# Weight loads moved behind a transpose, mixing ahead of the next products, and reciprocals on ScalarE, in a planned attention and GLU block

## Chip, cores and metric

The kernel runs on one core of a Trainium2 chip. The metric is the device time of one execution in microseconds (us); the time before is 262.38 us, the median of 3 runs (262.22 to 262.53).

## What is computed

```python
xn = layernorm(x)                                  # x: 2048 x 640
q, k, v = split_heads(xn @ wqkv)                   # 32 heads of 20
logits[h, s, w] = q[h, s] . k[h, s - 2 w] / sqrt(20), w = 0..7, masked where s < 2 w
attn = softmax(logits, axis=w)
o[h, s] = sum_w attn[h, s, w] * v[h, s - 2 w]
out = x + o @ wo + ((xn @ w_gate) * (xn @ w_up)) @ w_down   # 1536 hidden
```

All inputs and the output are bf16. Every position looks at eight positions only, so the attention itself is elementwise work and not a matrix product.

## The kernel before

The 2048 positions are cut into four chunks of 512 (c = 0 to 3). Features lie on the partitions, 5 tiles of 128; the 512 positions of a chunk are the free dimension. All matmuls of the projections, the gate/up part and the output are 128x128 weights against 128x512.

**Normalized input.** Chunk 0 takes a short way: its x comes in already turned, in two halves of 256 positions (`load_x0`, L139), TensorE sums over features with a matrix of ones (`feature_sums`, L246), VectorE subtracts the mean (`center`, L263), ScalarE squares (`squares`, L273) and takes the root by Ln and Exp (`roots`, L282), and the q and k projections run on the centered x and are scaled afterwards (`first`, L301). Chunks 1 to 3 come in row by row: VectorE takes the statistics (`stats`, L203), GpSimd the inverse root (L221 to L224), ScalarE scales (L233), SP stores the result xn in DRAM (`keep_xn`, L374) and reads it back with a DMA that transposes it into `xnT` (`turn_all`, L381).

**Projections** (`project`, L416): 10 groups of 5 matmuls give q and k, 5 groups give v; ScalarE casts each from PSUM (L450). k and v keep a halo of 14 positions of the chunk before, copied by GpSimd (L439).

**Gate and up** (`glu`, L667): per chunk 12 tiles f, each a gate group and an up group of 5 matmuls; ScalarE casts both (L679) and VectorE multiplies them to h(c, f) (L693).

**Attention** (`attention`, L634). VectorE multiplies q with k shifted, two offsets at a time (n = 0 to 3; `product`, L494), and adds five tiles to one (`fold`, L505 to L508). Two folds make one group g of four offsets: TensorE sums over the features of a head with a 128x32 matrix (`logits`, L520), ScalarE takes the exponential (`exps`, L529) into e, SP stores e in DRAM (`keep_e`, L541) and loads it back spread over the features of each head, as A(c, g) (`load_a`, L553). TensorE sums e over the offsets (`sums`, L565), VectorE takes the reciprocal (`inverse`, L577), and SP spreads it by way of DRAM as R(c). VectorE mixes: A times shifted v (`mix`, L608), added up (`gather`, L618), folded and multiplied with R to o(c) (`whole`, L626, L627).

**Down and output** (`finish`, L701): for each of 5 output tiles, 12 matmuls of w_down with all h(c, f) and 5 of wo with o(c) into one PSUM bank (L713, L718); VectorE adds x (L735), and GpSimd, in the last chunk SP, stores (L740). For chunk 3 all five down groups come first and the outputs after them.

**Order of the work.** Nothing is scheduled at run time. Each engine runs one list in order, and the class `Plan` (L27) makes these lists when the program is built. Every step is added with its engine, a cost in us that the author put down, the steps that it needs, a priority (lower first), rings (how many buffers there are, and which step frees one) and a slack added to its ready time. `run` (L56) takes, again and again, the engine that can start first and the ready step of lowest priority on it. A step on the same engine becomes ready `LAG` (0.2) after the end of what it needs. So a cost or a priority changes only the order in which instructions stand on an engine. The DMA issues of SP, ScalarE and GpSimd stand in the lists of these engines, and an engine that waits for a semaphore holds up everything behind it in its list.

Weights are loaded in blocks, `wa` and `wqkv` by SP and ScalarE (L167 to L177), `wgu`, `wd` and `wo` by GpSimd; each GpSimd load is held back by a tiny copy that reads one element of something earlier (`gate`, L183).

Of the kernel before, what the change touches and what calls it, by code (L numbers as in the profile page):

```python
# [7 lines left out]
BF = dt.bfloat16  # L8
# [18 lines left out]
class Plan:  # L27
# [8 lines left out]
    def __init__(self, rings):  # L36
        self.rings = {n: (k, []) for n, k in rings.items()}
        self.tasks = {e: [] for e in ("pe", "dve", "act", "pool", "sp")}
        self.done = {}
        self.start = {}  # L40
        self.free = {"pe": 2.9, "dve": 0.8, "act": 0.81, "pool": 1.6, "sp": 0.8}
        self.dma = 2.0
# [3 lines left out]

    def ready(self, t):
        _, _, name, _, _, need, ring, _, _, slack = t
        r = max((self.done.get(n, self.INF) for n in need), default=0.0) + slack
        for one in (ring,) if isinstance(ring, str) else ring or ():  # L50
            k, users = self.rings[one]
            if len(users) >= k:
                r = max(r, self.done.get(users[-k], self.INF))
        return r

    def run(self):  # L56
        while any(self.tasks.values()):
            best = None
            for e, ts in self.tasks.items():
                if not ts:  # L60
                    continue
                rs = [(self.ready(t), t) for t in ts]
# [12 lines left out]
            emit()  # L75
            self.start[name] = at
            self.free[e] = at + took
            self.done[name] = at + took + self.LAG
            if kb is not None:
                self.dma = max(self.dma, at + took + 0.7) + kb / 360.0  # L80
                self.done[name] = self.dma + 1.0
# [3 lines left out]
def tile_kernel(ctx: ExitStack, tc, x, xT, x0_in, wa_in, wqkv_in, wo_in, wgu_in, wd_in, sel_in, out):  # L85
# [37 lines left out]
    def warm_up(n):  # L123
        for _ in range(n):
            nc.tensor.matmul(wps[:, 0:P], lhsT=warm[:], rhs=warm[:], start=True, stop=True)

    warm_up(19)

    plan = Plan({"mm": 5, "lg": 1, "aux": 2, "pw": 1, "f": 4, "m": 2, "q": 2, "xnT": 2, "h": 24, "g": 4,
                 "xt": 6, "A": 1, "o": 1, "xr": 3, "osb": 4, "xn": 1})  # L130
    add = plan.add
    st = {c: {} for c in range(NCH)}

# [5 lines left out]
    def load_x0(eng, h, lo, hi):  # L139
        def emit():  # L140
            if (h, lo) == (0, 0):
                both = pool.tile([P, 2, KT, CS], BF, name="x0", tag="m", bufs=2)
                st[0]["xt"], st[0]["xd"] = both[:, 0], both[:, 1]
            eng.dma_start(out=st[0]["xt"][:, lo:hi, h * CS // 2 : (h + 1) * CS // 2], in_=x0_in[h, :, lo:hi, :])

        return emit
# [20 lines left out]
    for eng, q, name, dst, src, cut, kb in (  # L167
# [6 lines left out]
        ("sp", nc.sync, ("wb", 0), wqkv, wqkv_in, blocks(0, 2), 320),  # L174
        ("act", nc.scalar, ("wb", 2), wqkv, wqkv_in, blocks(2, 5), 480),
        ("sp", nc.sync, ("wv",), wqkv, wqkv_in, blocks(5, 10), 800),
# [20 lines left out]
    add("pool", ("wgu", 6), gated(wgu, wgu_in, blocks(6, FT), lambda: wqkv[:, 9, KT - 1, P - 1 :]), 1.2, [("wv",)], prio=order, kb=1920); order += 1  # L197
    add("pool", ("wd",), gated(wd, wd_in, slice(None), lambda: st[0]["f", 0][:, 0, 0:1]), 1.2, [("pw", 0, 0)], prio=order, kb=1920); order += 1
    add("pool", ("wo",), gated(wo, wo_in, slice(None)), 1.1, [("wd",)], prio=order, kb=800); order += 1
# [46 lines left out]
    def feature_sums(what, h, lo, hi):  # L246


        def emit():
            if lo == 0:  # L250
                st[0]["sum", what, h] = ps_aux.tile([P, CS // 2], F32, name="sum_" + what, tag="aux")
            a, b = HALVES[h]
            for i in range(lo, hi):
                nc.tensor.matmul(
                    st[0]["sum", what, h][:], lhsT=ones[:], rhs=st[0][what][:, i, a:b],
                    start=(i == 0), stop=(i == KT - 1),
                )
            if what == "xt" and h == 0:
                warm_up(6 if hi == KT else 2)

        return emit

    def center(h, lo, hi):  # L263
        def emit():
            a, b = HALVES[h]
            nc.vector.scalar_tensor_tensor(
                st[0]["xd"][:, lo:hi, a:b], wide(st[0]["sum", "xt", h][:], hi - lo), -1.0 / D,
                st[0]["xt"][:, lo:hi, a:b], op0=ALU.mult, op1=ALU.add,
            )

        return emit

    def squares(h, lo, hi):  # L273
        def emit():
            if (h, lo) == (0, 0):
                st[0]["sq"] = pool.tile([P, KT, CS], BF, name="sq", tag="o", bufs=1)
            a, b = HALVES[h]
            nc.scalar.activation(st[0]["sq"][:, lo:hi, a:b], st[0]["xd"][:, lo:hi, a:b], ACT.Square)

# [10 lines left out]
    def normalized(h):  # L290
        def emit():
            if h == 0:
                st[0]["xnT"] = pool.tile([P, KT, CS], BF, name="xnT", bufs=2)
            a, b = HALVES[h]
            nc.vector.tensor_tensor(  # L295
                st[0]["xnT"][:, :, a:b], st[0]["xd"][:, :, a:b], wide(rstd0[:, a:b], KT), ALU.mult
            )
# [3 lines left out]
    def first(h, j, hi, i=None):  # L301


        def emit():
            if i == 0 or (i is None and h == 1):
                st[0]["ps0", j] = ps_main.tile([P, 2, CS // 2], F32, name="ps0", tag="mm")
            a, b = HALVES[h]
            for n in range(2):
                for ii in range(KT) if i is None else (i,):
                    if (h == 0 and (i is None) == (n == 0)):  # L310
                        continue
                    nc.tensor.matmul(
                        st[0]["ps0", j][:, n, :], lhsT=(wqkv[:, j, ii, :] if n else wa[:, ii, j, :]),
                        rhs=st[0]["xd"][:, ii, a:b], start=(ii == 0), stop=(ii == KT - 1), skip_group_check=True,
                    )
# [72 lines left out]
    for c in range(1, NCH):  # L388
# [3 lines left out]
        for k in ks:  # L392
            add("dve", ("stats", c, k), stats(c, k), 1.1, [("xc", c), ("xn0", 1)], prio=c * 100 - 110)
        add("pool", ("root", c), root_pool(c, ks), 2.2, [("stats", c, k) for k in ks], prio=c * 100)
# [239 lines left out]
    def attention(c, prio, mprio):  # L634
        halves = ((0, CS // 2), (CS // 2, CS)) if c == 0 else ((0, CS),)
        for n in range(W // 2):
            g = n // 2
            for lo, hi in halves:
                add("dve", ("pwh", c, n, lo), product(c, n, lo, hi), 2 * KT * (hi - lo) / 1920 + 0.08,
                    [("qk", c, lo)] + ([("pwh", c, n, 0)] if lo else []), prio=prio + (n if lo == 0 else n),  # L640
                    ring=("pw" if lo == 0 else None), until=("pw", c, n))
            add("dve", ("pw", c, n), fold(c, n), 2.3, [("pwh", c, n, halves[-1][0])], prio=prio + n - 0.5, ring="f", until=("logits", c, g))
        for g in range(2):
            add("pe", ("logits", c, g), logits(c, g), 0.3, [("pw", c, 2 * g + 1), ("pw", c, 2 * g), ("sel",)], prio=-100,
                ring="lg", until=("exp", c, g))
            add("act", ("exp", c, g), exps(c, g), 0.6, [("logits", c, g)], prio=-100)
            if c == 0 and g == 1:
# [4 lines left out]
                ring="A" if g == 0 else None, until=("m", c, W // 2 - 1))  # L652
        add("pe", ("sums", c), sums(c), 0.15, [("exp", c, 0), ("exp", c, 1)] + ([("mask", c)] if c == 0 else []), prio=-100,
            ring="aux", until=("rs", c))
        add("dve", ("rs", c), inverse(c), 1.3, [("sums", c)], prio=-50)
        add("sp", ("kept r", c), keep_r(c), 0.65, [("rs", c)], prio=-100, kb=64)
        add("sp", ("R", c), load_r(c), 0.65, [("kept r", c)] + ([("o", c - 1)] if c else []), prio=-100, kb=128)
        for n in range(W // 2):
            add("dve", ("m", c, n), mix(c, n), 2.75, [("A", c, n // 2), ("v", c)], prio=mprio + n,
                ring="m", until=("mm", c, n + 1) if n < W // 2 - 1 else ("o", c))  # L660
            if n:
                add("dve", ("mm", c, n), gather(c, n), 2.75, [("m", c, n)], prio=mprio + n)
        add("dve", ("o", c), whole(c), 2.85, [("mm", c, W // 2 - 1), ("R", c)], prio=mprio + 9, ring="o", until=("pe fin", c, KT - 1))

# [36 lines left out]
    def finish(c, prio):  # L701
        for m in range(KT):
# [68 lines left out]
    for c in range(NCH):  # L771
# [4 lines left out]
        finish(c, 500 + 100 * c)  # L776
        attention(c, 100 * c, 100 * c + 150)
    plan.run()
# [56 lines left out]
```

## Time and profile before

| | |
|---|---|
| median of 3 runs | 262.38 us |
| the profiled execution's own time | 261.74 us |
| its span, first to last instruction | 260.0 us |
| granted TensorE clock over the span | 1.0 |
| VectorE busy | 229.8 us |
| ScalarE busy | 104.6 us |
| DMA | 27.10 MB, mean 104 GB/s |
| mean of a 128x512 gate/up matmul (L673) | 379 ns, one every 216 ns |
| product (L494), mix (L608), gather (L618), each 128x5120 | 2.8 us |
| reciprocal (L577) | 951 ns, 4 times |

All times inside the execution are microseconds from the start of the span. In the rows of the timeline the first number is the start, the second the time from the first start to the last end of the merged instructions, then engine, line, operation, tiles and shape, the count, and in brackets the idle time before it with what ended it. PE is TensorE's matmuls, PEld its weight loads, DVE VectorE, ACT ScalarE, POOL GpSimd, SP the engine that only issues DMAs. In the rows of a group, the numbers after the bar are busy time and mean duration, and after the second bar the idle time before. Matmuls overlap, so their durations don't add up; the starts do.

### The profile page before, as it was taken

What the parts mean: (1) busy time and instruction counts of PE and PEld (TensorE: products, weight loads), DVE (VectorE), ACT (ScalarE), POOL (GpSimd) and SP (SyncE); (2) the same over time, 40 slices, a digit from 0 to 9 for tenths busy, and PEclk for the clock granted to TensorE, in tenths of its full rate; (3) what the DMA queues carried; (4) which work ended last, traced back from release to release, by engine and by line L of the source; (5) the groups of instructions that cost most, each with busy time, mean ns of one, the idle gap of its engine ahead of it and who ended that gap; (6) DMA issues with size and microseconds to landing.
All of it is one profiled execution on the core that took longest, in us unless ns stands there. A gap on an engine that the chain in (4) does not pass through costs nothing.

```text
span 260.0 us, 3329 instructions
## 1 busy us (share of the span) xinstructions
PE 253.0 (97%) x1275; PEld 121.6 (47%) x1298; DVE 229.8 (88%) x235; ACT 104.6 (40%) x178; POOL 37.8 (15%) x67
## 2 busy tenths in 40 slices
PE   8999999999999999999999999999999999999994
PEld 6784444434444444444444444444444444444462
DVE  2599789972999999999999999999999989999813
ACT  3415595559555564525045645520035554000000
POOL 0302800022100000317040002003040000031000
PEclk9999999999999999999999999999999999999999
DMA  6993198305650000511540001502115004020002
GB/s 217 402 426 147 33 347 281 75 24 199 218 91 16 7 0 24 191 55 65 182 107 12 1 25 35 190 20 77 45 49 179 2 13 151 20 81 40 23 0 101
DMA packets 17503, 27.10 MB, mean 104 GB/s; under 512 B 9584, under 2 KB 13296, under 8 KB 17104
## 3 DMA queue, kind: packets, MB, share of 16 engines
q1 hardware_dynamic: 13664, 14.18, 17.3%
q0 software_dynamic: 2336, 11.31, 11.8%
q10 hardware_dynamic: 1488, 1.41, 1.6%
q8 instruction: 10, 0.16, 0.3%
q14 instruction: 5, 0.04, 0.1%
HBM read 19.16 MB, written 5.77 MB: 96 GB/s over the span
## 4 chain that ended last, share of the span: by engine, by line
PE 84%; DVE 6%; DMA 3%; POOL 2%; ACT 2%; issue 1%; ACTq 1%
PE psf L713 20%; PE ps L429 19%; PE psu L673 17%; PE psg L673 17%; PE psf L718 8%; DMA wqkv<-wqkv 3%; PE lps L520 1%; DVE stats L210 1%; DVE xnT L295 1%; POOL rstd L222 1%; ACT x_c L233 1%; DVE pw L494 1%; POOL rstd L221 1%; DVE q L331 0%; DVE k L331 0%
## 5 line engine op out<-in xcount | busy, mean ns | idle before, releaser
L673 PEld LDWEIGHTS <-wgu 128*128 128x128 bf16 x480 | 46.6, 98 | 56.5 <-issue 0.7
L673 PE MATMUL psu<-xnT,wgu 128*128 128x512 bf16 x234 | 59.3, 379 | 0.3
L673 PE MATMUL psg<-xnT,wgu 128*128 128x512 bf16 x235 | 59.4, 379 | 0.3
L713 PE MATMUL psf<-hT,wd 128*128 128x512 bf16 (+1 forms) x246 | 54.1, 369 | 0.3
L608 DVE TENSOR_TENSOR m<-v,A 128x5120 bf16<-128x5120 bf16 x16 | 44.9, 2814 | 6.0 <-DMA A<-eD 6.0
L494 DVE TENSOR_TENSOR pw<-q,k 128x5120 bf16<-128x5120 bf16 (+1 forms) x20 | 45.6, 2284 | 0.0
L679 ACT CAST us<-psu 128x512 bf16<-128x512 f32 x48 | 28.1, 586 | 31.1 <-PE psu L673 30.9
L429 PE MATMUL ps<-xnT,wqkv 128*128 128x512 bf16 x170 | 40.0, 379 | 0.3
L679 ACT CAST gs<-psg 128x512 bf16<-128x512 f32 x48 | 28.2, 587 | 27.5 <-PE psg L673 27.5
L713 PEld LDWEIGHTS <-wd 128*128 128x128 bf16 x252 | 24.6, 98 | 27.4 <-issue 0.2
L618 DVE TENSOR_TENSOR m<-m 128x5120 bf16<-128x5120 bf16 x12 | 33.8, 2817 | 0.0
L429 PEld LDWEIGHTS <-wqkv 128*128 128x128 bf16 x175 | 17.0, 98 | 20.4 <-issue 0.2
L718 PE MATMUL psf<-o,wo 128*128 128x512 bf16 (+1 forms) x104 | 24.2, 369 | 0.1
L693 DVE TENSOR_TENSOR hT<-gs,us 128x512 bf16<-128x512 bf16 x48 | 19.6, 418 | 3.3 <-ACT us L679 3.2
L740 POOL DMA_DIRECT2D out<-osb x15 | 8.2, 549 | 78.5 <-DVE osb L735 78.2
L505 DVE TENSOR_TENSOR pw<-pw 128x2048 bf16<-128x2048 bf16 x16 | 19.5, 1217 | 0.0
L429 PE MATMUL ps<-xnT,wa 128*128 128x512 bf16 x75 | 18.5, 380 | 0.0
L450 ACT CAST v<-ps 128x512 bf16<-128x512 f32 x20 | 11.6, 586 | 14.0 <-PE ps L429 14.0
L718 PEld LDWEIGHTS <-wo 128*128 128x128 bf16 x105 | 10.3, 98 | 11.3
L233 ACT ACTIVATE x_c<-x_c,mrstd,rstd 128x640 bf16<-128x640 bf16 x12 | 10.8, 922 | 9.3 <-POOL mrstd L224 9.3
L450 ACT CAST q<-ps 128x512 bf16<-128x512 f32 x15 | 8.8, 584 | 7.5 <-PE ps L429 7.5
L506 DVE TENSOR_TENSOR pw<-pw 128x1024 bf16<-128x1024 bf16 x16 | 11.1, 692 | 0.5
(85 smaller groups left out, 170.2 us busy)
## 6 DMA issues: line engine op xcount, KB each, us to landing
A<-eD SPq DMA_DIRECT2D x8, 512.0 KB, 4.5
x_c<-x SPq DMA_DIRECT2D x3, 640.0 KB, 8.5
wgu<-wgu POOLq DMA_DIRECT2D x1, 1920.0 KB, 11.1
wd<-wd POOLq DMA_DIRECT2D x1, 1920.0 KB, 8.8
xnD<-x_c SPq DMA_DIRECT2D x3, 640.0 KB, 5.4
xr<-xT POOLq DMA_DIRECT2D x15, 128.0 KB, 4.2
out<-osb POOLq DMA_DIRECT2D x15, 128.0 KB, 2.0
wgu<-wgu POOLq DMA_DIRECT2D x1, 1280.0 KB, 7.3
```

The lines of the kernel that those rows point to most:

```text
L233: nc.scalar.activation(st[c]["x", k], st[c]["x", k], ACT.Identity, bias=b, scale=r)
L429: nc.tensor.matmul(ps[:, 0 : hi - lo], lhsT=weight(b, i), rhs=s["xnT"][:, i, lo:hi], start=(i == 0), stop=(i == KT - 1),)
L450: nc.scalar.copy(dst[:, t, o + lo : o + hi], s["ps", b, lo][:, 0 : hi - lo])
L494: nc.vector.tensor_tensor(s["pw", n][:, :, :, lo:hi], s["q"][:, None, :, lo:hi].to_broadcast([P, 2, KT, hi - lo]), pairs(s["k"][:, :, off ...
L505: nc.vector.tensor_tensor(t[:, :, 0:2, :], t[:, :, 0:2, :], t[:, :, 2:4, :], ALU.add)
L608: nc.vector.tensor_tensor(s["m", n][:], pairs(s["v"][:, :, off : off + CS], DIL), s["A"][:, 2 * n : 2 * n + 2, None, :].to_broadcast([P, 2 ...
L618: nc.vector.tensor_tensor(b[:], a[:], b[:], ALU.add)
L673: nc.tensor.matmul(ps[:], lhsT=wgu[:, f, r, i, :], rhs=st[c]["xnT"][:, i, :], start=(i == 0), stop=(i == KT - 1))
L679: nc.scalar.copy(t[:], st[c]["gps", f, r][:])
L693: nc.vector.tensor_tensor(h[:], st[c]["gu", f, 0][:], st[c]["gu", f, 1][:], ALU.mult)
L713: nc.tensor.matmul(ps[:], lhsT=wd[:, f, m * P : (m + 1) * P], rhs=st[c]["h", f][:, lo:hi], start=(f == 0), stop=False)
L718: nc.tensor.matmul(st[c]["psf", m, lo][:], lhsT=wo[:, t, m * P : (m + 1) * P], rhs=st[c]["o"][:, t, lo:hi], start=False, stop=(t == KT - 1))
```

## The change

1. The first half and the second half of chunk 0's x, of its centered form and of its squares each get a tile of their own, so that a row of a half is contiguous; before, a half was a strided part of a row of 512.
2. The load of block 2 to 4 of `wqkv` moves from ScalarE's queue to SP's, and there are 22 warm-up matmuls instead of 19.
3. The load of `wd` waits for the transpose of chunk 1 (`turned`) instead of chunk 0's first fold; `wo` follows it.
4. Mixing of chunks 0 to 2 gets a priority ahead of the products of the next chunk (100 c + 50 instead of 100 c + 150, where the next chunk's products have 100 c + 100).
5. The reciprocal of the sums becomes exp(-ln(s)) by two ScalarE activations instead of a VectorE reciprocal.
6. In the planner, logits get a slack of 0.8 and sums one of 0.6; several costs are raised; a step that needs one on its own engine isn't charged the lag; statistics of chunks 2 and 3 get a later priority; the last chunk's down waits in the plan for the end of chunk 2's output; two entries are put into ring "m".

```diff
-    def ready(self, t):
+    def ready(self, e, t):
...
-        r = max((self.done.get(n, self.INF) for n in need), default=0.0) + slack
+        r = max((self.done.get(n, self.INF) - (self.LAG if self.by.get(n) == e else 0.0) for n in need), default=0.0) + slack
...
-    warm_up(19)
+    warm_up(22)
...
+    plan.rings["m"][1].extend([("xn0", 1), ("kept", 1)])
...
-                both = pool.tile([P, 2, KT, CS], BF, name="x0", tag="m", bufs=2)
-                st[0]["xt"], st[0]["xd"] = both[:, 0], both[:, 1]
-            eng.dma_start(out=st[0]["xt"][:, lo:hi, h * CS // 2 : (h + 1) * CS // 2], in_=x0_in[h, :, lo:hi, :])
+                both = pool.tile([P, 2, 2, KT, CS // 2], BF, name="x0", tag="m", bufs=2)
+                for n in range(2):
+                    st[0]["xt", n], st[0]["xd", n] = both[:, 0, n], both[:, 1, n]
+            eng.dma_start(out=st[0]["xt", h][:, lo:hi, :], in_=x0_in[h, :, lo:hi, :])
...
-        ("act", nc.scalar, ("wb", 2), wqkv, wqkv_in, blocks(2, 5), 480),
+        ("sp", nc.sync, ("wb", 2), wqkv, wqkv_in, blocks(2, 5), 480),
...
-    add("pool", ("wd",), gated(wd, wd_in, slice(None), lambda: st[0]["f", 0][:, 0, 0:1]), 1.2, [("pw", 0, 0)], prio=order, kb=1920); order += 1
+    add("pool", ("wd",), gated(wd, wd_in, slice(None), lambda: st[1]["xnT"][:, KT - 1, CS - 1 :]), 1.2, [("turned", 1)], prio=order, kb=1920); order += 1
...
-            add("dve", ("stats", c, k), stats(c, k), 1.1, [("xc", c), ("xn0", 1)], prio=c * 100 - 110)
+            add("dve", ("stats", c, k), stats(c, k), 1.05, [("xc", c), ("xn0", 1)], prio=c * 100 - 180 if c > 1 else -10)
...
+            l = pool.tile([P, P], F32, name="ls", bufs=1)
             r = pool.tile([P, P], BF, name="rs", bufs=1)
-            with nc.allow_low_precision(reason="weights are bf16"):
-                nc.vector.reciprocal(r[:], st[c]["sps"][:])
+            nc.scalar.activation(l[:], st[c]["sps"][:], ACT.Ln)
+            nc.scalar.activation(r[:], l[:], ACT.Exp, scale=-1.0)
...
-            add("dve", ("pw", c, n), fold(c, n), 2.3, [("pwh", c, n, halves[-1][0])], prio=prio + n - 0.5, ring="f", until=("logits", c, g))
+            add("dve", ("pw", c, n), fold(c, n), 2.55, [("pwh", c, n, halves[-1][0])], prio=prio + n - 0.5, ring="f", until=("logits", c, g))
...
-            add("pe", ("logits", c, g), logits(c, g), 0.3, [("pw", c, 2 * g + 1), ("pw", c, 2 * g), ("sel",)], prio=-100,
-                ring="lg", until=("exp", c, g))
+            add("pe", ("logits", c, g), logits(c, g), 0.35, [("pw", c, 2 * g + 1), ("pw", c, 2 * g), ("sel",)], prio=-100,
+                ring="lg", until=("exp", c, g), slack=0.8)
...
-        add("dve", ("rs", c), inverse(c), 1.3, [("sums", c)], prio=-50)
+        add("act", ("rs", c), inverse(c), 0.5, [("sums", c)], prio=-50)
...
-                add("pe", ("pe down", c, m), down, 2.6, first, prio=prio, ring="mm", until=("res", c, m))
+                add("pe", ("pe down", c, m), down, 2.6, first + [("pe fin", c - 1, KT - 1)], prio=prio, ring="mm", until=("res", c, m))
...
-        attention(c, 100 * c, 100 * c + 150)
+        attention(c, 100 * c, 100 * c + (50 if c < NCH - 1 else 150))
```

In the built program the orders differ as follows. On TensorE down and output of chunks 0, 1 and 2 stand behind 40, 57 and 78 of the 96 gate and up groups (before: 48, 69 and 96), so that the last 18 gate and up groups stand right before chunk 3's down. Chunk 1's projections begin behind 19 groups instead of 23. On VectorE the mixes of chunk c stand among or ahead of the products of chunk c + 1. On SP the load A(c, 0) of chunks 1 to 3 stands between the two stores of e instead of behind both and the store of the reciprocals.

More of the change, by code (lines that the diff above doesn't have):

```diff
@@ L39, in __init__ @@
         self.done = {}
+        self.by = {}
         self.start = {}
@@ L61, in run @@
                     continue
-                rs = [(self.ready(t), t) for t in ts]
+                rs = [(self.ready(e, t), t) for t in ts]
                 at = max(self.free[e], min(r for r, _ in rs))
@@ L78, in run @@
             self.done[name] = at + took + self.LAG
+            if kb is None:
+                self.by[name] = e
             if kb is not None:
@@ L251, in emit @@
                 st[0]["sum", what, h] = ps_aux.tile([P, CS // 2], F32, name="sum_" + what, tag="aux")
-            a, b = HALVES[h]
             for i in range(lo, hi):
                 nc.tensor.matmul(
-                    st[0]["sum", what, h][:], lhsT=ones[:], rhs=st[0][what][:, i, a:b],
+                    st[0]["sum", what, h][:], lhsT=ones[:], rhs=st[0][what, h][:, i, :],
                     start=(i == 0), stop=(i == KT - 1),
@@ L264, in emit @@
         def emit():
-            a, b = HALVES[h]
             nc.vector.scalar_tensor_tensor(
-                st[0]["xd"][:, lo:hi, a:b], wide(st[0]["sum", "xt", h][:], hi - lo), -1.0 / D,
-                st[0]["xt"][:, lo:hi, a:b], op0=ALU.mult, op1=ALU.add,
+                st[0]["xd", h][:, lo:hi, :], wide(st[0]["sum", "xt", h][:], hi - lo), -1.0 / D,
+                st[0]["xt", h][:, lo:hi, :], op0=ALU.mult, op1=ALU.add,
             )
@@ L275, in emit @@
             if (h, lo) == (0, 0):
-                st[0]["sq"] = pool.tile([P, KT, CS], BF, name="sq", tag="o", bufs=1)
-            a, b = HALVES[h]
-            nc.scalar.activation(st[0]["sq"][:, lo:hi, a:b], st[0]["xd"][:, lo:hi, a:b], ACT.Square)
+                both = pool.tile([P, 2, KT, CS // 2], BF, name="sq", tag="o", bufs=1)
+                st[0]["sq", 0], st[0]["sq", 1] = both[:, 0], both[:, 1]
+            nc.scalar.activation(st[0]["sq", h][:, lo:hi, :], st[0]["xd", h][:, lo:hi, :], ACT.Square)
         return emit
@@ L295, in emit @@
             nc.vector.tensor_tensor(
-                st[0]["xnT"][:, :, a:b], st[0]["xd"][:, :, a:b], wide(rstd0[:, a:b], KT), ALU.mult
+                st[0]["xnT"][:, :, a:b], st[0]["xd", h][:], wide(rstd0[:, a:b], KT), ALU.mult
             )
@@ L306, in emit @@
                 st[0]["ps0", j] = ps_main.tile([P, 2, CS // 2], F32, name="ps0", tag="mm")
-            a, b = HALVES[h]
             for n in range(2):
@@ L313, in emit @@
                         st[0]["ps0", j][:, n, :], lhsT=(wqkv[:, j, ii, :] if n else wa[:, ii, j, :]),
-                        rhs=st[0]["xd"][:, ii, a:b], start=(ii == 0), stop=(ii == KT - 1), skip_group_check=True,
+                        rhs=st[0]["xd", h][:, ii, :], start=(ii == 0), stop=(ii == KT - 1), skip_group_check=True,
                     )
@@ L638, in attention @@
             for lo, hi in halves:
-                add("dve", ("pwh", c, n, lo), product(c, n, lo, hi), 2 * KT * (hi - lo) / 1920 + 0.08,
+                add("dve", ("pwh", c, n, lo), product(c, n, lo, hi), 2 * KT * (hi - lo) / 1920 + 0.15,
                     [("qk", c, lo)] + ([("pwh", c, n, 0)] if lo else []), prio=prio + (n if lo == 0 else n),
                     ring=("pw" if lo == 0 else None), until=("pw", c, n))
-            add("dve", ("pw", c, n), fold(c, n), 2.3, [("pwh", c, n, halves[-1][0])], prio=prio + n - 0.5, ring="f", until=("logits", c, g))
+            add("dve", ("pw", c, n), fold(c, n), 2.55, [("pwh", c, n, halves[-1][0])], prio=prio + n - 0.5, ring="f", until=("logits", c, g))
         for g in range(2):
-            add("pe", ("logits", c, g), logits(c, g), 0.3, [("pw", c, 2 * g + 1), ("pw", c, 2 * g), ("sel",)], prio=-100,
-                ring="lg", until=("exp", c, g))
+            add("pe", ("logits", c, g), logits(c, g), 0.35, [("pw", c, 2 * g + 1), ("pw", c, 2 * g), ("sel",)], prio=-100,
+                ring="lg", until=("exp", c, g), slack=0.8)
             add("act", ("exp", c, g), exps(c, g), 0.6, [("logits", c, g)], prio=-100)
@@ L652, in attention @@
                 ring="A" if g == 0 else None, until=("m", c, W // 2 - 1))
-        add("pe", ("sums", c), sums(c), 0.15, [("exp", c, 0), ("exp", c, 1)] + ([("mask", c)] if c == 0 else []), prio=-100,
-            ring="aux", until=("rs", c))
-        add("dve", ("rs", c), inverse(c), 1.3, [("sums", c)], prio=-50)
+        add("pe", ("sums", c), sums(c), 0.25, [("exp", c, 0), ("exp", c, 1)] + ([("mask", c)] if c == 0 else []), prio=-100,
+            ring="aux", until=("rs", c), slack=0.6)
+        add("act", ("rs", c), inverse(c), 0.5, [("sums", c)], prio=-50)
         add("sp", ("kept r", c), keep_r(c), 0.65, [("rs", c)], prio=-100, kb=64)
@@ L658, in attention @@
         for n in range(W // 2):
-            add("dve", ("m", c, n), mix(c, n), 2.75, [("A", c, n // 2), ("v", c)], prio=mprio + n,
+            add("dve", ("m", c, n), mix(c, n), 2.83, [("A", c, n // 2), ("v", c)], prio=mprio + n,
                 ring="m", until=("mm", c, n + 1) if n < W // 2 - 1 else ("o", c))
             if n:
-                add("dve", ("mm", c, n), gather(c, n), 2.75, [("m", c, n)], prio=mprio + n)
-        add("dve", ("o", c), whole(c), 2.85, [("mm", c, W // 2 - 1), ("R", c)], prio=mprio + 9, ring="o", until=("pe fin", c, KT - 1))
+                add("dve", ("mm", c, n), gather(c, n), 2.83, [("m", c, n)], prio=mprio + n)
+        add("dve", ("o", c), whole(c), 2.95, [("mm", c, W // 2 - 1), ("R", c)], prio=mprio + 9, ring="o", until=("pe fin", c, KT - 1))
     def glu(c, prio):
```

## The prediction, made before the changed kernel was run

> **What bounds it now.** I read the page first. TensorE is busy 253.0 of 260.0 us and carries 84% of the chain that ended last, at full clock; VectorE is busy 88%.
>
> ```profile
> span 260.0 us, 3329 instructions
> PE 253.0 (97%) x1275; PEld 121.6 (47%) x1298; DVE 229.8 (88%) x235; ACT 104.6 (40%) x178; POOL 37.8 (15%) x67
> PE 84%; DVE 6%; DMA 3%; POOL 2%; ACT 2%; issue 1%; ACTq 1%
> ```
>
> So TensorE's list sets the end, and the change removes none of it. What can be won is only time in which TensorE doesn't start a matmul at its pace (five 128x512 in 1.08 us, 0.216 each). From the first projection matmul (18.97) to the end of the last output matmul (256.14) there are 1,070 x 0.2158 = 230.9 us of matmuls (1,053 whole ones, and 34 half-width ones counted as 17), 8 logit passages and 4 passages of the sums. The timeline of TensorE shows passages with and without a wait:
>
> ```profile
> 38.49 0.39 PE L520 MATMUL lps<-f,sel 128*32 128x512 bf16 x2
> 39.10 0.39 PE L520 MATMUL lps<-f,sel 128*32 128x512 bf16 x2 [0.22 <-DVE f L508]
> 39.42 1.25 PE L673 MATMUL psu<-xnT,wgu 128*128 128x512 bf16 x5
> ```
>
> ```profile
> 132.92 0.40 PE L520 MATMUL lps<-f,sel 128*32 128x512 bf16 x4
> 133.25 1.04 PE L673 MATMUL psg<-xnT,wgu 128*128 128x512 bf16 x4
> ```
>
> At 133 the change from the last big matmul before to the first after takes 0.64, a fixed price of 0.43 over a matmul's 0.216 (a passage of the sums costs 0.32). At 38.5 it takes 1.24: 0.60 is waiting for the fold `f`. Measured in the same way 52.2 loses 0.41, 94.9 loses 0.26, 80.3 loses 0.10, the other four nothing: **1.37 us** in all. 230.9 + 8 x 0.43 + 4 x 0.32 + 1.37 = 237.0 of the 237.2 measured, so there is hardly another gap. The start has three:
>
> ```profile
> 3.45 0.58 PE L254 MATMUL sum_xt<-x_114,ones 128*128 128x256 bf16 x2 [0.26 <-DMA x_114<-x]
> ...
> 8.87 0.71 PE L254 MATMUL sum_xt<-x_114,ones 128*128 128x256 bf16 x5 [0.53 <-DMA x_114<-x]
> ...
> 11.31 1.53 PEld L312 LDWEIGHTS <-wqkv 128*128 128x128 bf16 x15 [0.38 <-DMA wqkv<-wqkv]
> ```
>
> By starts, 8.07 to 8.87 is 0.69 over a matmul's 0.109 (second half of x0 not there), 10.94 to 11.32 is 0.27 over (block 2 of `wqkv`). Behind the last matmul 3.6 us of residual and store remain, which the change leaves.
>
> **Part by part.**
>
> *Start.* The half x0 tiles become contiguous, so a row goes in one packet (1,024, 1,536, 2,560 bytes) instead of 512-byte pieces. The DMA view of 5 to 7 us:
>
> ```profile
> q1 hardware_dynamic: 173, 0.39, 53.1%
> q10 hardware_dynamic: 370, 0.20, 34.4%
> ```
>
> q10 carries x0's second half in 512-byte packets, q1 the weights in larger ones. [...] q10 gets half as many bytes: 320 KB (0.33 MB) at 0.10 MB/us takes 3.3 us. Like q1's packets it would move 0.39 MB in 53.1% of 2 us, 0.37 MB/us alone, half of that shared: 1.8 us, 1.5 sooner. Needed is 0.69. [...] Block 2 of `wqkv` moves from ScalarE's queue to SP's, behind blocks 0 and 1. It [...] needs about 480 KB / 0.37 = 1.3 us after about 7.2, landing near 9 with lag; needed 10.3. The 0.27 goes. SP has one more issue (0.33 to 0.69) ahead of `wqkv`'s v part and the x load of chunk 1, which landed at 13.74 and is used at 20.26: nothing. First half of x0: 0.15 sooner perhaps, but wa's last blocks landed at 6.89, just when they would then be needed: 0. Three more warm-up matmuls (3 x 0.107) end at 3.30, ahead of 3.45: 0. Centering and squares keep rows of 512 elements (681 and 614 ns): 0. Gain **0.96**, bounds 0.3 and 1.2.
>
> *Reciprocals.* From VectorE go 4 x 0.95. ScalarE gets Ln and Exp on 128 elements each.
>
> ```profile
> L341 ACT ACT_TABLE_LOAD x1 | 1.3, 1283 | 3.1 <-issue 3.1
> L285 ACT ACTIVATE rstd_113<-sum_sq,eps 128x256 f32<-128x256 f32 x2 | 0.9, 464 | 1.4 <-PE sum_sq L254 1.4
> L286 ACT ACTIVATE rstd_113<-rstd_113 128x256 f32<-128x256 f32 x1 | 0.4, 417 | 0.0
> ```
>
> At most 0.46 + 0.42 at half that width: 0.7 per chunk, ScalarE is 40% busy. [...] But the row shows one load, after which Ln, Exp, and later the logits' Exp all run: no switch, so 0.7. VectorE isn't the bound, so its 3.8 us are slack. What the pair delays: R's store, and A(c,1) behind it on SP; neither ends late below.
>
> *Weights later.* wd and wo (2.7 MB) were issued at 30.55 and 31.22 and landed 8.8 and 11.0 us later, over chunk 1's store of xn:
>
> ```profile
> wd<-wd POOLq DMA_DIRECT2D x1, 1920.0 KB, 8.8
> xnD<-x_c SPq DMA_DIRECT2D x3, 640.0 KB, 5.4
> ...
> wo<-wo POOLq DMA_DIRECT2D x1, 800.0 KB, 11.0
> ```
>
> That store took 35.55 to 42.83 (7.3; the shortest of the three 3.5), then the transposes ran from 42.83 and their packets ended at 47.4. Alone I expect 35.55 + 3.5 to 4.3 + 4.6, 43.7 to 44.5. The new order asks for it earlier: 19 gate/up groups instead of 23 stand before chunk 1's projections, so need is at 18.97 + 5.40 + 19 x 1.079 + 0.43 = 45.3. Margin 0.8 to 1.6. On POOL the gate now blocks the copies of k's and v's halo, wo's issue and chunk 2's rstd until about 44; the first user of those is at 56 or later. wd then lands by about 53 and wo by 56; first use at 95.7.
>
> *Mixing first, slack.* In the new order the logits stand one group later or more. The first: 14 groups instead of 13, 39.5, fold ready at 39.1. The second: 52.9, and the fold before it loses one stats group (1.04) and one or two h products (0.34 each): about 51.5 instead of 52.8. For the rest I summed VectorE's new list by its rows' pace (products, mixes and gathers 2.74, fold 2.6, h 0.34, residual 0.60, whole o 3.0) against TensorE's, both on the clock of before. Chunk 0's o, for example: the last q of chunk 1 is cast at 59.5; product, fold and one h end at 65.3 (A(0,0) landed near 63); four mixes and three gathers 19.2, the second product 2.74, nine h 3.1, o itself 3.0: 93.3, needed at 98.3. In the same way fold (1,1) is ready at 96, its passage at 99.3; (1,3) 111 against 114.5; (2,1) 152 against 157; (2,3) 165 against 168.5; (3,1) 206 against 208.3; (3,3) 220 against 221.5. The outputs o of chunks 1 and 2: 141 against 152, 196.5 against 199.9. Chunk 2's xnT: 73 against 75.2. On SP the load A(c,0) now stands between the two stores of e, and chunk 3's x load behind chunk 2's transposes; the x load has over ten us to its use. A(1,1) and A(2,0) land about when VectorE gets to them (124 and 167), which costs VectorE 1 us at most and TensorE nothing; the last A is rival D. The planner's new costs and ring entries only order; they emit nothing. So the 1.37 goes; I leave 0.07 for a late one: **1.3**, bounds 0.8 and 1.37.
>
> *Sum.* Profiled execution 261.74 = 260.0 + 1.74 outside; minus 0.96 and 1.3 is 259.5. The median of the runs, 262.38, is 0.64 above it; I carry that over: **260.1**.
>
> **Rivals.**
>
> A. *No new wait*: 260.1, by its bounds 259.8 to 261.3. For it: TensorE's list is unchanged and the margins above are positive.
>
> B. *The start doesn't yield*: [...] x0 lands near 8.5 and `wqkv` as before: 262.38 - 1.3 - 0.3 = 260.8. [...]
>
> C. *A wait takes the place*: chunk 1's transposes are late for the projections at 45.3. Half late (0.8 to 1.5 us): about 261.2. If the weights weren't what slowed the store and it takes 11.9 us as now, 35.55 + 11.9 = 47.4, a wait of 2.1: 262.2, no change. Against it: the shortest store took 3.5.
>
> D. *Slower, at the tail*. Down of chunk 2 now comes early (197), so chunk 3's last gate/up groups stand right before down of chunk 3, with no 18 us of other matmuls between. Let E be the last logit passage (221.5). Down starts at E + 14.8 and needs h 10 and 11 of chunk 3 at E + 16.9 and 17.2. They stand on VectorE behind the mix of A(3,1): exp, store of e (3.7 by 55.28 to 59.0), load of A (4.0 to 4.5, by 59.0 to 63.1) put A at about E + 9.2; mix 2.74, two h, gather 2.74 make h 10 and 11 ready at about E + 16.3. The cover is 0.8 us. Every us later than A at E + 10.2 costs TensorE one; slower than before begins at 3 us (E + 13.2). A 4 us lateness gives 263. For it: A loads took up to 5.8 beside xr loads. Against it: here nothing else is on the queues but rD.
>
> E. *Logits wait again* elsewhere by about 1 us: 261.2.
>
> **Numbers.** A 0.62, B 0.13, C 0.15 (a third of it no change), D 0.05, E 0.05. Forecast 260.1. Range 259.6 to 261.6: it takes in A, B, E and half-late C, with the runs' scatter (0.15) beyond the bounds, and leaves out the rest. About 0.2% (0.5 us) is what a measurement of this kernel can tell from no change; faster 0.89, same 0.06, slower 0.05.
>
> **What would show it.** Right: no idle time before the second sums of x0 and before `wqkv`'s block 2, the first v projection near 18.0; eight passages near 0.64; the store of chunk 1's xn landing in about 4 us and the first q/k matmul of chunk 1 near 44.3 without a wait; ScalarE's pair at about 0.7 and one table load; the last matmul near 253.8. Wrong: a gap before the first matmul of chunk 1's projections (C), a gap inside the last down with VectorE idle before the third mix of chunk 3 (D), a fold as releaser of a logit passage (E). A second table load would refute the price of the reciprocals.

## The result and the profile after

| | before | after |
|---|---|---|
| median | 262.38 us | 259.94 us (259.44 to 260.57, 4 runs) |
| ratio, 95% interval | | 0.9908 (0.9886 to 0.9931) |
| span of the trace shown | 260.0 | 258.4 |
| own time of that execution | 261.74 us | about 260.15 (an estimate) |
| first v matmul to last matmul, by starts | 18.97 to 256.03: 237.06 | 18.94 to 254.63: 235.69 |
| behind the last matmul's start, in the span | 3.94 | 3.75 |
| outside the span | 1.77 | 1.74 to 1.81 in the four runs |

The forecast was 260.1, faster. The four runs of after have spans of 257.7, 258.1, 258.2 and 258.8; the trace (258.38) is of a further execution, and with 1.74 to 1.81 outside it took about 260.15. The one profile of the last experiment fell in a disturbed execution (266.61 us) and isn't read.

The page of after, first the lines that answer to those of before:

```profile
span 258.4 us, 3317 instructions
...
PE 251.8 (97%) x1278; PEld 121.5 (47%) x1301; DVE 227.7 (88%) x231; ACT 105.9 (41%) x186; POOL 41.1 (16%) x67
...
PE 95%; DMA 2%; issue 1%; SPq 0%; DVE 0%
```

VectorE left the chain (6% before, 0% now). ScalarE's and GpSimd's shares of it (2% each) went as well. DMA keeps 2% (3% before), nearly all in one piece at the start, the load of `wa`. TensorE's timeline of after shows where both come from:

```profile
3.62 0.59 PE L258 MATMUL sum_xt<-x_117,ones 128*128 128x256 bf16 x2
...
7.12 0.27 PE L314 MATMUL ps_156<-x_117,wa 128*128 128x256 bf16 x1
8.01 0.28 PE L314 MATMUL ps_148<-x_117,wa 128*128 128x256 bf16 x1 [0.62 <-DMA wa<-wa]
...
9.11 0.71 PE L258 MATMUL sum_xt<-x_117,ones 128*128 128x256 bf16 x5
...
38.36 1.24 PE L676 MATMUL psu<-xnT,wgu 128*128 128x512 bf16 x5
39.53 0.40 PE L522 MATMUL lps<-f,sel 128*32 128x512 bf16 x4
39.87 1.25 PE L676 MATMUL psg<-xnT,wgu 128*128 128x512 bf16 x4
...
44.19 1.24 PE L676 MATMUL psg<-xnT,wgu 128*128 128x512 bf16 x5
45.27 1.03 PE L431 MATMUL ps<-xnT,wa 128*128 128x512 bf16 x4
```

At 39.53 a logit passage stands without a bracket (the idle time before a row), and so do the other seven: each costs 0.64 from big matmul to big matmul. Chunk 1's projections start at 45.27, just behind the last gate group. In this execution the start has only changed its wait. The second sums (9.11) have no bracket now, and block 2 of `wqkv` none either, but the fourth row of `wa`'s matmuls does: by starts 7.12 to 8.01 is 0.78 over a matmul's 0.109.

The DMA view of 5 to 7 us shows part of the reason. Its columns are packets, MB and the share of 16 engines' time:

```profile
q1 hardware_dynamic: 141, 0.33, 62.9%
q10 hardware_dynamic: 109, 0.25, 31.0%
```

q10 (x0) moves 0.25 MB instead of 0.20 in fewer, larger packets, as foreseen. q1 (the weights) falls from 0.39 to 0.33, though its share of time grew from 53.1% to 62.9%: its packets were slower, by these rows 143 ns each instead of 98, not only fewer. That fall is this execution's; the seven other profiles with the new start have 0.36 to 0.50 on q1 beside 0.24 to 0.29 on q10. `wa`'s last blocks landed at 7.96; before, at 6.89.

The page's DMA rows of after, with the median from issue to landing at the end:

```profile
xnD<-x_c SPq DMA_DIRECT2D x3, 640.0 KB, 4.6
wd<-wd POOLq DMA_DIRECT2D x1, 1920.0 KB, 8.0
```

The store that mattered, chunk 1's, went from 35.52 to 39.00: 3.5 us instead of 7.3. Its transposes were issued from 39.02.

ScalarE's groups (busy and mean ns behind the first bar):

```profile
L343 ACT ACT_TABLE_LOAD x1 | 1.3, 1283 | 2.1 <-issue 2.1
...
L580 ACT ACTIVATE rs<-ls 128x128 bf16<-128x128 f32 x4 | 1.2, 310 | 0.1
L579 ACT ACTIVATE ls<-sps 128x128 f32<-128x128 f32 x4 | 1.1, 283 | 0.0
```

One table load, and 0.59 us for a pair.

### The profile page after: what moved, and what is told of

It is laid out like the page before. It is cut to its first block, busy times and chain, and to the rows that moved or that the text cites. A ratio compares the mean times of both kernels' runs of the same rounds, so it can differ in the third digit from the quotient of the medians.

```text
span 258.4 us, 3317 instructions
## 1 busy us (share of the span) xinstructions
PE 251.8 (97%) x1278; PEld 121.5 (47%) x1301; DVE 227.7 (88%) x231; ACT 105.9 (41%) x186; POOL 41.1 (16%) x67
## 4 chain that ended last, share of the span: by engine, by line
PE 95%; DMA 2%; issue 1%; SPq 0%; DVE 0%
PE ps L431 21%; PE psf L716 20%; PE psg L676 20%; PE psu L676 20%; PE psf L721 8%; DMA wa<-wa 2%; PE lps L522 1%; PE ps_299 L314 0%; PE ps_287 L314 0%; PE ps_262 L314 0%; PE ps_246 L314 0%; PE ps_275 L314 0%; PE sum_sq L258 0%; PE ps_148 L314 0%; PE sps L567 0%
## 5 line engine op out<-in xcount | busy, mean ns | idle before, releaser
L531 ACT ACTIVATE e<-lps 128x512 bf16<-128x512 f32 x8 | 4.8, 599 | 46.5 <-PE lps L522 46.5
L441 POOL COPY v<-v 128x70 bf16<-128x70 bf16 x3 | 6.2, 2050 | 41.6 <-ACT us L682 28.9
```

## The experiments

My theory after this profile: 1.37 us come from the logit passages, and it takes the slack, the mixing order and the late weights together to get them. The rest comes from the start, where the wait moved to `wa`. Rivals: one part alone does it; the start is worth nothing, as the two profiles say; the reciprocals help. "Body" below is the time from the first v matmul's start to the last matmul's. A planner makes every list anew, so an undone part also takes along what the planner then puts elsewhere.

**1. The old start under the new order.** Changed kernel with before's tiles for x0, before's queue for block 2 and 19 warm-ups:

```diff
-    warm_up(22)
+    warm_up(19)
...
-        ("sp", nc.sync, ("wb", 2), wqkv, wqkv_in, blocks(2, 5), 480),
+        ("act", nc.scalar, ("wb", 2), wqkv, wqkv_in, blocks(2, 5), 480),
...
```

> The changed kernel with the start of before: x0's halves as strided parts of a tile of 512, block 2 of wqkv on ScalarE's queue, 19 warm-up matmuls. Theory 1 (the start gave nothing: the wait for x0 only moved to the last blocks of wa, and all the gain is the logits' waits): as long as the changed kernel within 0.3 us, about 260.0, first v matmul near 18.97, waits of 0.69 before the second sums of x0 and 0.27 before block 2 of wqkv. Theory 2 (the start gains 0.96 as predicted, the profiled execution was an unlucky one): 0.7 to 1.0 us longer than the changed kernel.

Measured: 260.69 us (11 runs), 0.9943 (0.9926 to 0.9959). Body 235.69, first v matmul 18.96; in its trace the second sums waited 0.81 by starts for x0, and block 2 was in time. Everything but the start thus brings its 1.37 us: 0.57% (0.41 to 0.74) of 262.4 is 1.5 us (1.1 to 1.9).

**2. x0 behind wa.** Changed kernel, the second half of x0 issued by SP behind `wa`'s last blocks:

```diff
-        ("act", nc.scalar, ("x0", 1, 0), None, (1, 0, 5), None, 320),
+        ("sp", nc.sync, ("x0", 1, 0), None, (1, 0, 5), None, 320),
```

> The changed kernel with the second half of x0 issued by SP behind wa's last blocks instead of by ScalarE[...]. Theory 1 (wa's last blocks are late because x0's second half, now in large packets, takes half of the turns): wa lands near 7 instead of 7.96, the wait of 0.78 in the first 25 matmuls goes, x0 lands before 8.2; first v matmul near 18.0 to 18.3, 0.6 to 1.0 us shorter. Theory 2 (one slow DMA engine sets the landing, whoever takes turns): wa still lands near 8, no gain beyond 0.3.

Measured: 260.01 us (6 runs), 0.9917 (0.99 to 0.9934). TensorE's timeline of this kernel:

```profile
5.56 2.94 PE L314 MATMUL ps<-x,wa 128*128 128x256 bf16 x25
8.34 0.71 PE L258 MATMUL sum_xt<-x,ones 128*128 128x256 bf16 x5
```

All 25 matmuls on `wa` run through, and the second sums follow at once: 0.77 sooner than in after. `wa`'s last blocks landed at 6.09. This speaks for the order of the bytes, not their sum, as what made the wait in after; one execution doesn't settle it, since number 5 issues these loads as after does and had no wait there either. The first v matmul came at 18.16. Yet the median is that of after.

**3. Slack alone.** Kernel before, with the two slacks and nothing else:

```diff
-                ring="lg", until=("exp", c, g))
+                ring="lg", until=("exp", c, g), slack=0.8)
...
-            ring="aux", until=("rs", c))
+            ring="aux", until=("rs", c), slack=0.6)
```

> The kernel before with the slack for logits (0.8) and sums (0.6) alone. If slack is what removes the logits' waits: the four waits of together 1.37 us go, 261.0 (1.2 to 1.4 shorter than before). If the freed VectorE and the mixing order are needed for it: waits stay or move, within 0.5 of before.

Measured: 264.27 us (6 runs), 1.0073 (1.0054 to 1.0093). Slower than before: body 238.99. TensorE's waits of this kernel (total, times, longest):

```profile
PE lps L520 <- DVE f L508: 1.1, 2, 0.9
...
PE psf L713 <- DVE hT L693: 0.4, 1, 0.4
```

By starts the passages still lose 0.61, 0.12, 0.26, 1.30 and 0.44. Slack only tells the planner to place a passage later; the fold `f` still comes late in VectorE's list, and a down group now waits for an `hT`.

**4. The new start alone**, on the kernel before (tiles, queue of block 2, 22 warm-ups; the reverse of the diff of 1).

> The kernel before with the new start alone (contiguous halves of x0, block 2 of wqkv on SP, 22 warm-up matmuls). Theory 1: 262.4, no change within 0.3; a wait of about 0.8 for wa in place of the waits of 0.69 and 0.27. Theory 2: 261.4, first v matmul near 18.0.

Measured: 261.9 us (22 runs), 0.998 (0.9969 to 0.999): 0.5 us (0.26 to 0.8) of 262.4. The logit waits of before are all there, and one is longer: 0.60, 0.40, 0.48 and 0.26 against 0.60, 0.41, 0.10 and 0.26, with a body of 237.42 against 237.06. Its profiled execution started late (first v matmul 19.52): 0.63 and 0.36 were waits for `wa`, and its clock record begins, at full speed, only at 6.36 (in after at 4.87, where the warm-up matmuls go from one every 0.107 us to one every 0.056).

**5. Weights early.** Changed kernel, the same lists, but `wd` and `wo` issued by GpSimd right after chunk 1's statistics, with no gate:

```diff
-    add("pool", ("wd",), gated(wd, wd_in, slice(None), lambda: st[1]["xnT"][:, KT - 1, CS - 1 :]), 1.2, [("turned", 1)], prio=order, kb=1920); order += 1
+    add("pool", ("wd",), lambda: None, 1.2, [("turned", 1)], prio=order, kb=1920); order += 1
...
+            if c == 1:
+                nc.gpsimd.dma_start(out=wd[:], in_=wd_in)
+                nc.gpsimd.dma_start(out=wo[:], in_=wo_in)
```

> The changed kernel, every engine's list as it is, but with wd and wo issued by GpSimd right behind chunk 1's inverse roots (about 29.7, as before the change) instead of behind the transpose. If these loads are what slowed the store of chunk 1's xn: the store takes about 7 us again instead of 3.5, the transposes end near 47.4, and TensorE waits 2.0 to 2.4 us before the first matmul of chunk 1's projections (45.3): 262.0 to 262.4. If it was something else: as the changed kernel, 260.0.

Measured: 262.25 us (11 runs), 1.0016 (0.9988 to 1.0044), no difference from before. TensorE's timeline:

```profile
43.48 1.24 PE L679 MATMUL psg<-xnT,wgu 128*128 128x512 bf16 x5
46.19 1.25 PE L434 MATMUL ps<-xnT,wa 128*128 128x512 bf16 x5 [1.47 <-DMA xnT<-xnD]
```

This is the wait of rival C, 1.63 us by starts, at the very matmul that it named. The store took 6.3 us here instead of 3.5. Without the late weights the earlier place of chunk 1's projections costs what the order wins. That the late weights alone would gain nothing is argued, not run: in before these projections began at 50.2, behind the transposes' end at 47.4.

**6. No slack.** Changed kernel without the two slacks (the reverse of the diff of 3).

> The changed kernel without the slack for logits and sums, everything else planned anew. If the slack takes the waits away: logits wait again, 0.5 to 1.4 us in all, 260.5 to 261.4. If the order of VectorE and the raised costs do: 260.0.

Measured: 264.98 us (4 runs), 1.0099 (1.0073 to 1.0124), body 240.13: waits of 0.61 and 1.10 at the logits, and 2.53 by starts inside gate and up at 123.3. TensorE's waits and ScalarE's timeline of this kernel:

```profile
PE psg L676 <- ACT q L452: 2.4, 1, 2.4
...
PE lps L522 <- DVE f L510: 0.9, 2, 0.7
```

```profile
124.61 0.92 ACT L238 ACTIVATE x_c<-x_c,mrstd,rstd 128x640 bf16<-128x640 bf16 x1 [5.70 <-POOL mrstd L229]
125.44 0.56 ACT L452 CAST q<-ps 128x512 bf16<-128x512 f32 x1
```

The big one is a head-of-line wait: ScalarE stood 5.70 us before a scaling of chunk 3's x, which needs GpSimd's mean (ready at 124.57). The cast of q, which frees a bank of PSUM (TensorE's output memory) for the gate group, stood behind it. In after the same scaling starts at 120.95 with 2.58 of idling, and no bank is missing. So this figure is the price of a whole other list and not of the slack alone.

**7. Mixing late.** Changed kernel with the old priority of mixing:

```diff
-        attention(c, 100 * c, 100 * c + (50 if c < NCH - 1 else 150))
+        attention(c, 100 * c, 100 * c + 150)
```

> The changed kernel with mixing behind the next chunk's products as before (priority 100 c + 150). If TensorE's list without waits is all that counts, and slack gives it: 260.0 with eight logit passages of 0.64. If mixing first is needed to keep VectorE's folds and o in time: waits of 0.5 to 2 us, 260.5 to 262.

Measured: 265.91 us (4 runs), 1.0134 (1.0105 to 1.0164), body 240.92. TensorE's timeline and the table by stages (the columns at the end are the granted clock, DMA share and GB/s):

```profile
128.23 0.39 PE L522 MATMUL lps<-f,sel 128*32 128x512 bf16 x2
131.12 0.48 PE L522 MATMUL lps<-f,sel 128*32 128x512 bf16 x2 [2.50 <-DVE f L510]
131.53 4.31 PE L716 MATMUL psf<-hT,wd 128*128 128x512 bf16 x12
```

```profile
127.00:131.00 4.00, 1.62 (x9) 0.49 (x7) 3.93 (x6) 0.00 (x0) 1.09 (x2) 1.00 0.18 57
131.00:135.00 4.00, 3.88 (x11) 1.38 (x11) 4.00 (x5) 0.60 (x1) 1.08 (x2) 0.57 0.28 88
135.00:139.00 4.00, 4.00 (x20) 1.83 (x19) 3.93 (x5) 0.00 (x0) 1.07 (x2) 1.00 0.13 52
```

One passage loses 2.98 by starts. Then twelve matmuls take 4.31 us where twelve take 2.75 elsewhere, 1.56 more: the granted clock was 0.57 over these 4 us. As in number 6 this is the price of another list.

**8. Reciprocals on VectorE.** Changed kernel with before's reciprocal:

```diff
-            nc.scalar.activation(l[:], st[c]["sps"][:], ACT.Ln)
-            nc.scalar.activation(r[:], l[:], ACT.Exp, scale=-1.0)
+                nc.vector.reciprocal(r[:], st[c]["sps"][:])
...
-        add("act", ("rs", c), inverse(c), 0.5, [("sums", c)], prio=-50)
+        add("dve", ("rs", c), inverse(c), 1.3, [("sums", c)], prio=-50)
```

> The changed kernel with the reciprocal on VectorE as before, planned anew. If VectorE isn't the bound, as I said: 260.0 within 0.3, VectorE busy 231. If the 3.8 us were needed: waits for folds or for h, 260.5 or more.

Measured: 259.9 us (4 runs), 0.9909 (0.9892 to 0.9926), body 235.69, no logit wait, VectorE busy 230.9 instead of 227.7. They are worth nothing here.

**9 and 10. After, and x0 behind wa, head to head.**

> The changed kernel once more, in the same call as the version that issues the second half of the block behind TensorE's small-weight loads, so that the two are timed on one chip. The body from the first v matmul to the last matmul should again be 235.69 us (it was that in four kernels). If the start varies from execution to execution with the landing of the small-weight loads, this profile should show its first v matmul anywhere from 18.2 to 19.5 us; if the start is fixed by the instruction order, at 18.94 +- 0.1 as in the first profile. Time 259.9 to 260.2 us, 0.990 to 0.992 of before.

> The changed kernel with the second half of the first block issued by SP behind the small-weight loads, timed head to head with the changed kernel. Theory 'the wait moved from the block to the small weights': first v matmul again near 18.2 us, 0.75 us ahead of the changed kernel's first profile, and the median 0.3 to 0.7 us below the changed kernel's in the same call. Rival 'the landing scatters whatever the order': medians within 0.2 us, and the first v matmul may lie anywhere from 18.2 to 19.

Measured: 260.1 us, 0.9912 (0.9896 to 0.9928), and 260.24 us, 0.9921 (0.9903 to 0.9938), 6 runs each. First v matmul 18.94 and 18.38, body 235.69 in both. In these two executions 0.48 of the 0.56 is given back behind the last matmul (3.76 against 4.24); likewise 3.75 in after against 4.25 in number 2. Number 2's theory of a faster median falls, and no version beat after. The last residual and the stores follow the last matmul at the same distance; what differs is the close of the program behind them. It doesn't go with the start: number 5 started at 18.22 and closed in 3.76, number 7 at 19.04 and closed in 4.24. Why the sooner start of these two kernels doesn't show in their medians stays open.

**11. A loaded twice.** Changed kernel, the last A loaded twice one behind the other, for rival D; the output is the same.

```diff
-                nc.sync.dma_start(
+            for _ in range(2 if (c, g) == (NCH - 1, 1) else 1):
+                nc.sync.dma_start(
```

> The changed kernel with the second half of the last chunk's A loaded twice into the same buffer, the second load behind the first, so that the last third of the last chunk's mixing starts later by one load (4 to 5 us); the output is unchanged. The tail rival of the prediction priced this chain at 1 us per us beyond its cover. By the traced cover (the eleventh down product's operand ready at 237.56 and needed at 238.5, about 1 us), TensorE should wait 3 to 4 us inside the last chunk's down and the time be 262.9 to 264 us. If the planner's order or the output's own tail hides more of it, the wait stays under 2 us and the time under 262 us.

Measured: 264.55 us (262.85 to 265.14, 11 runs), 1.0071 (1.0052 to 1.009). VectorE's and TensorE's timeline of this kernel:

```profile
234.31 2.83 DVE L612 TENSOR_TENSOR m<-v,A 128x5120 bf16<-128x5120 bf16 x1 [4.57 <-DMA A<-eD]
...
240.46 0.75 DVE L697 TENSOR_TENSOR hT<-gs,us 128x512 bf16<-128x512 bf16 x2
```

```profile
236.22 2.32 PE L717 MATMUL psf<-hT,wd 128*128 128x512 bf16 x10
240.93 11.26 PE L717 MATMUL psf<-hT,wd 128*128 128x512 bf16 x48 [2.39 <-DVE hT L697]
```

The third mix of chunk 3 starts at 234.31 instead of 230.40, 3.91 later, and the eleventh down matmul waits 2.55 by starts (238.38 to 240.93). Its turn came 0.12 sooner here than in after (238.50), so the cover is 3.91 + 0.12 - 2.55 = 1.5. After's trace says the same: the operand of the eleventh is ready at 236.97. The 237.56 that I had read for it before this run is the twelfth's; the prediction had 0.8. So the wait fell short of what I expected. The time did not: the body grew by 4.35. The stages behind the wait, as above:

```profile
240.90:242.00 1.10, 1.07 (x4) 0.39 (x4) 1.10 (x2) 0.00 (x0) 0.00 (x0) 0.74 0.00 0
242.00:243.00 1.00, 1.00 (x4) 0.40 (x3) 1.00 (x1) 0.00 (x0) 0.00 (x0) 0.50 0.00 0
...
244.00:245.00 1.00, 1.00 (x4) 0.40 (x3) 1.00 (x1) 0.00 (x0) 0.00 (x0) 0.58 0.00 0
245.00:246.00 1.00, 1.00 (x7) 0.42 (x5) 1.00 (x1) 0.00 (x0) 0.00 (x0) 1.00 0.00 0
```

For over 3 us four matmuls are counted in a us instead of seven: 4.35 - 2.55 = 1.8 us more. Four of the 11 runs kept a mean clock of 0.997 to 0.999 and took 262.85 to 263.58; the other seven had 0.991 to 0.993 and took 264.4 to 265.1.

**12. The old start once more.**

> The changed kernel with the start of before, once more: the new start alone (before with the new start) gave 0.998 of before, and the changed kernel gained 0.3% more than with the old start, but the profiles of one execution each show the first v matmul at 18.94 and 18.96. Theory 'the start is worth half a microsecond or more in the median, and the first profiles of the old start were lucky': ratio again 0.993 to 0.996, and in this profile the first v matmul stands at 18.9 to 19.5 us, not below 18.8. Rival 'the two starts scatter alike': ratio 0.990 to 0.992, as the changed kernel. The body is 235.69 us in either.

Measured: 260.76 us (7 runs), 0.992 (0.9901 to 0.9938). The ratio lies between those of number 1 and after, and its interval overlaps both, so it settles nothing that number 4 had not.

## Why the prediction was right, and where it was not

**Logits: right.** The body shrank by 237.06 - 235.69 = 1.37, the whole of what was measured in before; I had taken 1.3. The margins worked out from VectorE's list held: no passage waits in any kernel with after's order (numbers 1, 2, 5, 9, 10, 11), nor in number 8. Slack alone is slower than before (number 3), and so is the change without its slack or without its mixing order (numbers 6 and 7). Those two made new lists with new waits elsewhere, so they show that each is needed in this set and not what each is worth. Mixing first alone and the planner's raised costs and other new settings by themselves were not run.

**Weights: right.** The need at 45.3 was 45.27. The store took 3.5, the lower end of 3.5 to 4.3, and there was no wait. Number 5 shows what the zero stood on: when the weights come early, rival C's wait is real, 1.63 us.

**Reciprocals: right.** 0.59 per pair against "0.7", no second table load. Leaving them on VectorE would have made no difference: number 8 (259.9) is the same as after (259.94) within its interval.

**Start: the step that failed.** The term of 0.96 held two landings, and neither came as said. The first v matmul was to stand near 18.0 and the last matmul near 253.8; they stood at 18.94 and 254.63.

The trace marks the landing of a load in 16 parts, and TensorE starts right behind the last (8.83 and 8.87 for x0 before, 7.96 and 8.01 for `wa` in after). I had worked with the rate of a whole load:

| parts landed | before | after | x0 behind `wa` (numbers 2 and 10) |
|---|---|---|---|
| x0's second half: 12 of 16, last | 8.36, 8.83 | 7.08, 9.03 | |
| `wa`'s last blocks: 8 of 16, last | 5.87, 6.89 | 6.19, 7.96 | 5.55, 6.09 and 5.54, 6.13 |

*x0, 1.5 sooner.* Twelve parts came 1.3 sooner, the last one 0.2 later. Without the wait for `wa` the second sums could have run at 8.33 but would have waited for x0 until about 9.07, so in this execution the larger packets had not taken away even that wait. In the seven other profiles with the new start the last part came at 7.25 to 8.72, with the old start (before, numbers 1 and 3) at 8.83 to 9.15. Block 2 of `wqkv` landed at 10.23 where I had said near 9, still ahead of its need.

*wa, at zero.* "wa's last blocks landed at 6.89, just when they would then be needed: 0" took over a landing from a trace in which x0 had small packets. In after TensorE stands 0.78 for these blocks, and its first matmul on `wa` comes 0.14 later (5.54 against 5.40) where I had 0.15 sooner. Together that is 0.92 of the 0.96 that was to be won, and the gain in this execution is 0.03 (18.97 against 18.94). With the new start the last part of `wa` came at 7.07 to 8.54 in eight profiles, and TensorE waited for `wa` in seven; with the old start at 6.79 to 7.44 in three, with one wait (0.31, number 3). With x0 behind `wa` half of the parts are in 0.64 sooner (5.55 against 6.19), so x0's packets did delay `wa` in after. That its last part comes over 1 us behind the one before in some executions (8.54 and 7.27 in number 4, 8.09 and 6.80 in number 6) and not in others (7.07 and 6.86 in number 5, which had no wait) stays unexplained, and it decides how long TensorE waits.

The row of 5 to 7 us before holds 370 packets of q10 against 173 of q1, so the two did not alternate packet by packet, and "half of that shared" was a guess. By the medians of the traces five packets of 512 bytes take 135 ns and one of 2,560 takes 102: 24% less, where my 1.8 us instead of 3.3 is 45% less.

The first v matmul scatters with this start from 18.22 to 19.52 in eight profiles, so one profile can't price it. By the medians of number 4 the start is worth 0.5 (0.26 to 0.8): within the bounds of 0.3 to 1.2 (the lower one was my estimate), half of the value.

**Sum: right, in part by luck.** Numbers 1 and 4 give 1.5 (1.1 to 1.9) and 0.5 (0.26 to 0.8), 2.0 of the 2.44 measured, which lies within their bounds. The traces give less: from 261.74 to about 260.15 it is 1.6, of which 1.37 is the body. The traced execution of before was 0.64 below its median, that of after about 0.2 above; I carried the 0.64 over, and it was not there. That made up for what the start fell short of. Part of it can be seen: with before's lists the logit waits differ from execution to execution (1.37 in before, 1.72 in number 4), while after's order gave 235.69 in all five profiles of after and numbers 1, 2, 9 and 10. How often before's waits are longer no run shows.

**Rival D** did not come, and its price was too low: in number 11 the granted clock fell to 0.50 behind the wait of 2.55 us.

## What to carry to other kernels

Where a transfer is made to land sooner on one queue, work out again when the transfers of the other queues land, and go by the last part of each: here the wait for `wa`, of zero length in the trace of before, was 0.78 in that of after. A planner's settings can be worth something only together: here the set won 2.4 us, and it lost 2.6 and 3.5 against before with one of them taken out. Look at the medians before one profile prices a term below a microsecond.

## What the runs showed that I had not expected

In the traces of numbers 7 and 11 a wait of TensorE cost more than its length. The clock record of number 7 has half speed from 131.29 to 134.70, that of number 11 from 241.42 to 244.84: 3.4 us each, right behind the waits. In those of numbers 5 and 6 the clock stayed full behind theirs:

| run | wait by starts, us | granted clock behind it |
|---|---|---|
| 5 | 1.63 | 1.00 |
| 6 | 2.53 | 1.00 |
| 11 | 2.55 | 0.50 |
| 7 | 2.67 (without the slow passage) | 0.50 |

The two longest waits are the ones with the clock at half behind them, but 2.53 and 2.55 hardly differ, and these runs do not show what decides it.

The mean clocks of the runs show such losses too. In number 11 seven of 11 runs had a mean clock of 0.991 to 0.993, in number 7 three of 4 and in number 6 two of 4 had 0.993 or 0.994, and in number 5 three of 11 (263.57 to 264.84 us; its trace is of the fastest, 261.09). All other runs that are read here, before's too, had 0.997 or more. So the medians of these four numbers hold some of this price beside their waits.
